# Regrouping batch 1's attention and moving two weight loads around the end of block 0

## The chip, the cores and the metric

The kernel runs on one core of one Trainium2 chip. The metric is the device time of one execution in microseconds (us), taken as the median of several runs. Traces come from one profiled execution.

## What is computed

A retention attention over q, k and v of shape (8 batches, 8 heads, 576 positions, 64), followed by a feed-forward layer with a sine-squared activation. The reference, cut to what matters:

```python
scores = scale * np.matmul(q, k.transpose(0, 1, 3, 2))
Dmat = np.where(rel >= 0, gamma[:, None, None] ** rel[None, :, :], 0.0)
attn = np.matmul(scores * Dmat[None], v)              # (8, 8, 576, 64)
x = attn.transpose(0, 2, 1, 3).reshape(8 * 576, 512)
h = x @ w_in                                          # 512 -> 2048
g = h + np.sin(alpha * h) ** 2 / (alpha + 1e-9)
out = g @ w_out                                       # 2048 -> 512
```

All inputs and the output are float32; the kernel computes in float16 with float32 sums.

## The kernel before, in words

**Blocks and units.** The 4608 tokens are worked in nine blocks of 512. Blocks 0 to 7 hold the first 512 positions of batches 0 to 7, and block 8 the last 64 of all. Each block goes through 16 *units*, one for each 128 of the 2048 hidden columns. A unit is `project` (four matmuls into one PSUM bank, line 541), `sine` on ACT (line 549), `square` on ACT, DVE or POOL (lines 558, 560) and `product` on DVE (line 565), which also frees the bank. Blocks 0 and 1 then multiply by w_out in 16 steps of four matmuls, `gemm2(n, u, bank)` (line 587): u // 4 is the group of 128 output rows and u % 4 the quarter of w_out that is read. `finish` copies a row group out of PSUM on ACT or DVE and stores it with two DMAs from SP (line 580). Later blocks use another scheme for the second product (`Quarters`), whose weight sums are made by `weigh` on POOL (line 608).

**Attention of a batch.** It works in two halves p of 256 positions. `load` brings 512 KB of float32 of q, k or v (line 121). `cast` scales and rounds it to float16: k and q by a multiplication with decay factors (line 181) on DVE or POOL, v by a copy (lines 102, 104). k and q are then transposed, either on PE (`turn`, line 215, with `take`, lines 102 and 104, out of PSUM) or by a DMA from SP (`crossed`, line 205). On PE, `outer` forms the sums of k times v (line 298), `scores` the products of k and q (line 363), `values` the product of masked scores with v in two parts (line 406), and `add_states` adds the carried state (line 428). All of these are 64x64 tiles, where the rest of PE's work is 128x128. DVE masks the scores (`masked`, line 375), ACT evicts the sums (`evict`, line 102), and POOL carries them on (`more`, lines 344 and 345; `to_state`, line 332). `keep` writes the block's x on ACT. `relay=` names an engine that passes on a mark between the two parts of `values`.

**What sets the order.** The whole order is written out by hand in one list (lines 746 to 1481), and each engine works off its own instructions in that order. Waits come only from data and from the reuse of buffers and banks. PSUM is taken by name: `h0`, `h1`, `h2` and `op` are single banks, `m0` and `m1` pairs. Raw loads share six buffers.

**Queues.** All loads of q, k and v, all DMA transposes and all stores are issued by SP (queue q1 in the profile). The weights are loaded by POOL (queue q0), with a conversion to float16 on the way: `load_w_in(g)` (line 92) and `load_w_out(g)` (line 95), one quarter of 512 KB after conversion each.

**Around the change.** Block 0's units 4 to 15 stand at lines 859 to 914. Between their steps, DVE casts batch 1's first k (lines 870, 878), PE turns it (line 895), and POOL issues the second quarter of w_out (line 866). Then block 0's gemm2 steps alternate with batch 1's attention (lines 915 to 981). POOL issues the third and fourth quarters of w_out at lines 929 and 930. From line 982 batch 2's q is cast and transposed, and block 1's units begin at line 994.

Of the kernel before, what the change touches and what calls it, by code (L numbers as in the profile page):

```python
# [18 lines left out]
def kernel(  # L19
# [68 lines left out]
    V, A_, G_ = nc.vector, nc.scalar, nc.gpsimd  # L88
# [5 lines left out]
    def load_w_out(g):  # L94
        nc.gpsimd.dma_start(w_out16[:, 4 * g : 4 * g + 4, :], w_out_r[:, 4 * g : 4 * g + 4, :])
# [42 lines left out]
    def cast(b, nm, p, eng, ys=(0, 1)):  # L138
        t_ = raw[b, nm, p]
        if (b, nm, p) not in half:  # L140
            if p < 2:
                if nm == "k":
                    d_ = work.tile([P, 16 * D], F16, tag=f"k16{slot(b, p)}", bufs=1, name="k16")
                elif nm == "q":
                    n = order_of_q.index((b, p)) % 3 if b < 5 else 1 - p
                    d_ = work.tile([P, 16 * D], F16, tag=f"q16{n}", bufs=1, name="q16")
                else:
                    d_ = work.tile([P, 16 * D], F16, tag="v16", bufs=4, name="v16")
                d_ = (
                    d_.rearrange("p (h r d) -> p h r d", r=2, d=D)  # L150
                    if nm == "v"
                    else d_.rearrange("p (a r t d) -> p a r t d", a=4, r=2, t=2)
                )
            elif nm == "v":
                d_ = work.tile([P, H, D], F16, tag="vs16", bufs=B // 2, name="vs16")
            else:
                tag, n = ("qks16", 2) if b % 4 == 0 else (f"k16{int(nm == 'q')}", 1)
                d_ = work.tile([P, 4, 2, D], F16, tag=tag, bufs=n, name=nm + "s16")
            half[b, nm, p] = d_
        dst = half[b, nm, p]  # L160
        if p == 2:
            if nm == "v":
                copy(eng, dst.rearrange("p h d -> p (h d)"), t_.rearrange("p h d -> p (h d)"))
            else:
                eng.tensor_tensor(
                    dst.rearrange("p a t d -> p t a d"),
                    t_.rearrange("p (t a) d -> p t a d", t=2),
                    fac_s[nm].rearrange("p (t a) -> p t a", t=2).unsqueeze(3).to_broadcast([P, 2, 4, D]),
                    MULT,
                )  # L170
        elif nm == "v":
            h0, h1 = 4 * ys[0], 4 * ys[-1] + 4
            copy(
                eng,
                dst[:, h0:h1].rearrange("p h r d -> p (h r d)"),
                t_[:, h0:h1].rearrange("p h x -> p (h x)"),
            )
        else:
            a0, a1 = 2 * ys[0], 2 * ys[-1] + 2
            n = 2 * (a1 - a0)  # L180
            return eng.tensor_tensor(  # L181
                dst[:, a0:a1].rearrange("p a r t d -> p t (a r) d"),
                t_.rearrange("p (t a) x -> p t a x", t=2)[:, :, a0:a1].rearrange("p t a (r d) -> p t (a r) d", r=2),
                fac["halved k" if nm == "k" and b >= HALVED else nm]
                .rearrange("p (t x) -> p t x", t=2)[:, :, 2 * a0 : 2 * a1]
                .unsqueeze(3)
                .to_broadcast([P, 2, n, D]),
                MULT,
            )
# [19 lines left out]
    def turn(b, nm, p, tag, ys=(0, 1)):  # L209
        if (b, nm, p) not in trs:  # L210
            trs[b, nm, p] = psum.tile([P, 1024], F16, tag=tag, bufs=1, name="tr")
        tr, x = trs[b, nm, p], half[b, nm, p]
        for a in range(2 * ys[0], 2 * ys[-1] + 2):
            for r in range(2):
                matmul(  # L215
                    tr[:, 256 * a + 128 * r : 256 * a + 128 * r + 128],
                    x[:, a, r].rearrange("p t d -> p (t d)"),
                    ident,
                    start=(a == 0 and r == 0), stop=True, is_transpose=True, skip_group_check=True,
                )  # L220

    def take(b, nm, p, eng, ys=(0, 1)):
        d_ = new_T(b, nm, p).rearrange("p x n -> p (x n)")
        cols = slice(512 * ys[0], 512 * ys[-1] + 512)
        copy(eng, d_[:, cols], trs[b, nm, p][:, cols])
# [307 lines left out]
    def project(n, fc, tag, part=None):  # L533

        if n not in gT:
            gT[n] = work.tile([P, 2, FC, 256], F16, tag="gT", bufs=2, name="gT")
        if (n, fc) not in hps_of:
            hps_of[n, fc] = [bank(tag), None]
        cols = PART[part]
        for a in range(KT):  # L540
            matmul(  # L541
                hps_of[n, fc][0][:, cols], w_in16[:, a, fc * P : (fc + 1) * P], xs[n][:, a, cols],
                start=(a == 0 and part != 1), stop=(a == KT - 1), skip_group_check=True,
            )
# [9 lines left out]
    def square(n, fc, eng):  # L554
        s_t = hps_of[n, fc][1]
        ss_t = work.tile([P, 512], F16, tag="ss", bufs=4, name="ss_t")
        if eng is nc.scalar:
            nc.scalar.activation(ss_t, s_t, mybir.ActivationFunctionType.Square)  # L558
        else:
            eng.tensor_tensor(ss_t, s_t, s_t, MULT)  # L560
        hps_of[n, fc][1] = ss_t

    def product(n, fc):
        hps, ss_t = hps_of.pop((n, fc))
        nc.vector.scalar_tensor_tensor(  # L565
            gT[n][:, :, fc, :], ss_t.rearrange("p (t n) -> p t n", t=2), inva[:, fc : fc + 1],
            hps.rearrange("p (t n) -> p t n", t=2), MULT, ADD,
        )
# [13 lines left out]
    def gemm2(n, u, tag, cols=slice(0, 512)):  # L582
        c, part = divmod(u, 4)
        if (n, c, cols.start) not in ops:
            ops[n, c, cols.start] = psum.tile([P, 512], F32, tag=tag, bufs=1, name="ops")
        for fk in range(4 * part, 4 * part + 4):
            matmul(  # L587
                ops[n, c, cols.start][:, cols], gT[n][:, c // 2, fk, c % 2 * P : c % 2 * P + P], w_out16[:, fk, cols],
                start=(fk == 0), stop=(fk == FC - 1), skip_group_check=True,
            )  # L590
# [102 lines left out]
    at = [Attention(b) for b in range(B)]  # L693
# [52 lines left out]
    with tc.manual_schedule():  # L746
# [116 lines left out]
        project(0, 5, "m0")  # L863
        sine(0, 5)
        square(0, 5, A_)
        load_w_out(1)
        project(0, 6, "op")
        product(0, 5)
        product(0, 4)
        cast(1, "k", 0, V, (0,))  # L870
        sine(0, 6)
        square(0, 6, G_)
        project(0, 7, "h2")
        sine(0, 7)
        square(0, 7, A_)
        product(0, 6)
        product(0, 7)
        cast(1, "k", 0, V, (1,))
        project(0, 8, "h0")
        sine(0, 8)  # L880
        square(0, 8, G_)
# [2 lines left out]
        square(0, 9, A_)  # L884
        product(0, 8)
        product(0, 9)
        project(0, 10, "m0")
        sine(0, 10)
        square(0, 10, G_)
        project(0, 11, "op")  # L890
        sine(0, 11)
        square(0, 11, V)
        product(0, 10)
        product(0, 11)
        turn(1, "k", 0, "m1")
        project(0, 12, "h2")
        sine(0, 12)
        square(0, 12, G_)
        take(1, "k", 0, V, (0,))
        take(1, "k", 0, V, (1,))  # L900
        project(0, 13, "h0")
        sine(0, 13)
        square(0, 13, A_)
        cast(1, "q", 0, G_)
# [15 lines left out]
        gemm2(0, 0, "h0")  # L920
        at[0].to_state(3, G_)
        at[1].scores(0, 0, "m0")
        gemm2(0, 5, "op")
        at[1].scores(0, 1, "m1")
        at[1].masked(0, 0)
        at[1].masked(0, 1)
        cast(1, "v", 0, G_, (0,))
        cast(1, "v", 0, A_, (1,))
        load_w_out(2)
        load_w_out(3)  # L930
        gemm2(0, 13, "h2")
        load(2, "k", 1)
        load(2, "k", 0)
        load(2, "q", 0)
        at[1].outer((0,), "m0")
        at[1].evict((0,), A_)
        cast(1, "k", 1, G_)
        at[1].values(0, False, "m1", relay=G_)
        gemm2(0, 1, "h0")
        at[1].to_state(0, G_)  # L940
        at[1].values(0, True)
        turn(1, "k", 1, "h1")
        cast(1, "q", 1, V)
        take(1, "k", 1, V)
        at[1].add_states(0)
        at[1].keep(0, A_)
        load(2, "v", 0)
# [14 lines left out]
        cast(2, "k", 0, V)  # L962
        crossed(2, 0, "k")
        gemm2(0, 9, "h1")
        at[1].outer((1,), "m0")
        at[1].evict((1,), A_)
        at[1].more(2)
        at[1].to_state(2, G_)
        gemm2(0, 6, "op")
        gemm2(0, 14, "h2")  # L970
        at[1].values(1, False, "m1", relay=A_)
        gemm2(0, 2, "h0")
        at[1].values(1, True)
        at[1].add_states(1)
        at[1].keep(1, A_)
        gemm2(0, 10, "h1")
        gemm2(0, 15, "h2")
        finish(0, 3, V)
        weigh(1, 1, G_)
        gemm2(0, 7, "op")  # L980
        finish(0, 1)
        cast(2, "q", 0, V)
        crossed(2, 0, "q")
        crossed(2, 1, "k")
        load(3, "k", 1)
        at[1].more(3)
        at[1].to_state(3, G_)
        cast(2, "v", 0, G_)
# [10 lines left out]
        sine(1, 1)  # L999
        gemm2(0, 3, "h0")  # L1000
        product(1, 0)
        finish(0, 0)
        square(1, 1, A_)
        project(1, 2, "m1", 0)
# [507 lines left out]
```

## Time and profile before

| | |
|---|---|
| median of 3 runs | 297.12 us (296.72 to 297.46) |
| the profiled execution | 295.89 us |
| its span, from the first to the last instruction | 294.2 us |
| granted TensorE clock | 0.998 |
| moved by DMA | 49.89 MB, mean 170 GB/s |
| mean of one sine, square (ACT), product | 682, 630, 743 ns |

The profiled execution's own time is a little longer than its span, and 1.23 us below the median. In the profile, PE is TensorE's matmuls, PEld its weight loads, DVE VectorE, ACT ScalarE, POOL GpSimd and SP SyncE; SPq and POOLq are their DMA issues. A row of a timeline has its start, its length, engine, line, operation and tiles, and in brackets the idle time before it and what ended that. A duration of a matmul group includes the tail of its last one, so the start of the next group is the better measure. The DMA view has packets, megabytes and the share of the sixteen DMA engines' time for each queue.

### The profile page before, as it was taken

The numbers are of one execution on the slowest core, as the hardware profiler recorded it, in microseconds if no ns is written. First come the engines' busy times: TensorE is split into PE (matmuls) and PEld (weight loads), VectorE is DVE, ScalarE is ACT, GpSimd is POOL, SyncE is SP. The second block draws the span as 40 slices with busy tenths as digits, with TensorE's granted clock in tenths as the row PEclk, the third lists the DMA queues.
The fourth block names the chain that finished last, engine by engine and source line by source line (L and its number), as shares of the span: only waits on it lengthen the run. The fifth ranks groups of instructions, "written<-read, shape, count | busy, mean of one in ns | idle before, by whom it ended". The sixth has DMA issues, their size and how long they took to land.

```text
span 294.2 us, 8759 instructions
## 1 busy us (share of the span) xinstructions
PE 281.9 (96%) x3607; PEld 184.4 (63%) x3607; DVE 217.9 (74%) x298; ACT 209.0 (71%) x339; POOL 210.1 (71%) x201
## 2 busy tenths in 40 slices
PE   7799999999989999999999999999999999999993
PEld 5474454576544676666666666666666666665782
DVE  3759976899568799989686867686777495747861
ACT  2859732886847898877787778787868879887600
POOL 4888889999999989999979799679816800460000
PEclk9999999999999999999999999999999999999999
DMA  7999999999999378978797877667647201311225
GB/s 221 293 248 222 269 208 283 246 190 271 243 254 293 74 174 181 259 166 203 158 263 166 194 194 204 110 135 178 137 111 188 44 2 39 72 38 28 58 47 119
DMA packets 119159, 49.89 MB, mean 170 GB/s; under 512 B 69824, under 2 KB 118096, under 8 KB 119120
## 3 DMA queue, kind: packets, MB, share of 16 engines
q1 hardware_dynamic: 114528, 45.04, 64.1%
q0 software_dynamic: 4224, 4.19, 8.5%
q8 instruction: 28, 0.46, 0.7%
q10 hardware_dynamic: 368, 0.11, 0.2%
q14 instruction: 11, 0.09, 0.1%
HBM read 36.74 MB, written 9.44 MB: 157 GB/s over the span
## 4 chain that ended last, share of the span: by engine, by line
PE 77%; POOL 8%; DMA 5%; DVE 4%; SPq 2%; ACT 2%; issue 1%; POOLq 0%; ACTq 0%
PE hps L541 35%; PE hps L658 29%; PE ops L587 4%; POOL T L608 4%; DMA q<-in_q_dram 4%; PE sc L363 2%; PE o L406 2%; SPq L121 2%; DMA qT<-q 1%; DVE gT L565 1%; PE kv L298 1%; POOL q L181 1%; DVE ret L375 1%; PE tr L215 1%; POOL v L104 1%
## 5 line engine op out<-in xcount | busy, mean ns | idle before, releaser
L565 DVE SCALAR_TENSOR_TENSOR gT<-ss_t,inva,hps 128x512 f16<-128x512 f16 x144 | 105.4, 743 | 38.7 <-ACT ss_t L558 37.2
L549 ACT ACTIVATE s_t<-hps,alpha_t 128x512 f16<-128x512 f32 x144 | 96.7, 682 | 38.0 <-PE hps L541 37.4
L541 PE MATMUL hps<-xT,w_in 128*128 128x512 f16 (+1 forms) x600 | 121.1, 348 | 0.4 <-DVE gT L565 0.4
L541 PEld LDWEIGHTS <-w_in 128*128 128x128 f16 x664 | 63.5, 98 | 50.4 <-issue 1.1
L558 ACT ACTIVATE ss_t<-s_t 128x512 f16<-128x512 f16 x118 | 73.9, 630 | 3.3
L658 PEld LDWEIGHTS <-gT 128*128 128x128 f16 x656 | 63.8, 98 | 14.5
L630 POOL TENSOR_TENSOR gT<-gT,d 128x1024 f16<-128x1024 f16 x12 | 25.6, 2151 | 26.1 <-PE hps L658 24.7
L658 PE MATMUL hps<-T,gT 128*128 128x256 f16 x336 | 39.8, 273 | 0.0
L375 DVE TENSOR_TENSOR ret<-sc,mask 128x1024 f16<-128x1024 f32 (+1 forms) x32 | 35.1, 1118 | 4.3 <-PE sc L363 4.1
L658 PE MATMUL hps<-w_out,gT 128*128 128x256 f16 x320 | 38.2, 273 | 0.0
L678 DVE TENSOR_TENSOR osb<-osb,hps 128x512 f32<-128x512 f32 x35 | 23.9, 684 | 11.9 <-PE hps L658 11.3
L587 PE MATMUL ops<-w_out,gT 128*128 128x512 f16 x128 | 31.2, 380 | 0.0
L181 POOL TENSOR_TENSOR q<-q,cn 128x1024 f16<-128x1024 f32 (+1 forms) x16 | 26.2, 1649 | 0.1
L636 POOL TENSOR_TENSOR gT<-gT 128x1024 f16<-128x1024 f16 x12 | 25.3, 2129 | 0.0
L345 POOL TENSOR_TENSOR kvs<-s,kvs 128x256 f32<-128x256 f32 x24 | 19.1, 797 | 2.5 <-ACT kvs L102 0.8
L587 PEld LDWEIGHTS <-gT 128*128 128x128 f16 x128 | 11.6, 98 | 12.4
L332 POOL TENSOR_TENSOR s<-kvs,cn 128x256 f16<-128x256 f32 x23 | 16.1, 703 | 4.1 <-ACT kvs L102 3.3
L102 ACT CAST xT<-o 128x1024 f16<-128x1024 f32 (+1 forms) x15 | 14.4, 966 | 6.6 <-PE o L428 6.6
L181 POOL TENSOR_TENSOR k<-k,cn 128x1024 f16<-128x1024 f32 (+1 forms) x11 | 18.8, 1713 | 0.0
L102 ACT COPY osb<-hps 128x512 f32<-128x512 f32 (+2 forms) x15 | 8.2, 550 | 13.5 <-PE hps L658 13.3
L560 DVE TENSOR_TENSOR ss_t<-s_t 128x512 f16<-128x512 f16 x19 | 13.4, 708 | 5.7 <-ACT s_t L549 5.6
L344 POOL TENSOR_TENSOR s<-kvs,cn 128x256 f32<-128x256 f32 x24 | 16.3, 678 | 0.2
(76 smaller groups left out, 272.3 us busy)
## 6 DMA issues: line engine op xcount, KB each, us to landing
out_dram<-osb SPq DMA_DIRECT2D x70, 128.0 KB, 2.5
q<-in_q_dram SPq DMA_DIRECT2D x16, 512.0 KB, 5.6
k<-in_k_dram SPq DMA_DIRECT2D x10, 512.0 KB, 6.8
v<-in_v_dram SPq DMA_DIRECT2D x10, 512.0 KB, 6.2
k<-in_k_dram SPq DMA_DIRECT2D x24, 128.0 KB, 3.6
v<-in_v_dram SPq DMA_DIRECT2D x24, 128.0 KB, 3.4
w_in<-in_moe_w_in_dram POOLq DMA_DIRECT2D x4, 512.0 KB, 9.4
w_out<-in_moe_w_out_dram POOLq DMA_DIRECT2D x4, 512.0 KB, 10.6
```

The costliest lines, as they stand in the source:

```text
L102: eng.copy(d_, s_)
L181: return eng.tensor_tensor(dst[:, a0:a1].rearrange("p a r t d -> p t (a r) d"), t_.rearrange("p (t a) x -> p t a x", t=2)[:, :, a0:a1].rea ...
L375: made = nc.vector.tensor_tensor(ret.rearrange("p t (z x) -> p (t z) x", z=2)[:, :, 0:n], sc.rearrange("p t (z x) -> p (t z) x", z=2)[:, : ...
L541: matmul(hps_of[n, fc][0][:, cols], w_in16[:, a, fc * P : (fc + 1) * P], xs[n][:, a, cols], start=(a == 0 and part != 1), stop=(a == KT - ...
L549: nc.scalar.activation(s_t, hps, mybir.ActivationFunctionType.Sin, bias=0.0, scale=alpha_t[:, fc : fc + 1],)
L558: nc.scalar.activation(ss_t, s_t, mybir.ActivationFunctionType.Square)
L565: nc.vector.scalar_tensor_tensor(gT[n][:, :, fc, :], ss_t.rearrange("p (t n) -> p t n", t=2), inva[:, fc : fc + 1], hps.rearrange("p (t n) ...
L587: matmul(ops[n, c, cols.start][:, cols], gT[n][:, c // 2, fk, c % 2 * P : c % 2 * P + P], w_out16[:, fk, cols], start=(fk == 0), stop=(fk ...
L630: eng.tensor_tensor(self.part(0, 0, i), self.part(1, 1, i), self.d3[:, 4 * i : 4 * i + 4], SUB)
L636: eng.tensor_tensor(out_, self.part(1, 0, i), self.part(0, 0, i), SUB)
L658: matmul(self.ps[name][:, 256 * m + cols.start : 256 * m + cols.stop], left(j)[:, P * m : P * m + P], right(j)[:, cols], start=(tag is not ...
L678: nc.vector.tensor_tensor(out_, a, self.ps[ps], ADD)
```

## The change

Nothing is computed differently; instructions change places in the list.

- Units 6 to 13 of block 0: `load_w_out(1)` goes from ahead of unit 6 to behind its square. The two casts of batch 1's first k move later on DVE, by two products each. `load_w_out(2)` goes from line 929 to behind unit 10's square. The turn of k goes from ahead of unit 12 to behind unit 13's projection.
- Batch 1's attention: the two `scores` of half 0 stand together; the cast of the second k stands ahead of the outer product; the first `to_state` goes ahead of a gemm2 step, and the second part of `values` of half 0 stands with its `add_states`; in half 1 one gemm2 step goes ahead of the outer product, which then stands with the first part of `values`.
- `finish(0, 3)` copies on ACT instead of DVE. Batch 2's first q is cast on DVE behind unit 0's product, and its transpose and the load of batch 3's second k move with it, behind the transpose of batch 2's second k.

```diff
-        load_w_out(1)
         project(0, 6, "op")
         product(0, 5)
         product(0, 4)
-        cast(1, "k", 0, V, (0,))
         sine(0, 6)
         square(0, 6, G_)
+        load_w_out(1)
         project(0, 7, "h2")
...
         product(0, 7)
-        cast(1, "k", 0, V, (1,))
+        cast(1, "k", 0, V, (0,))
...
         product(0, 9)
+        cast(1, "k", 0, V, (1,))
         project(0, 10, "m0")
         sine(0, 10)
         square(0, 10, G_)
+        load_w_out(2)
...
         product(0, 11)
-        turn(1, "k", 0, "m1")
...
+        project(0, 13, "h0")
+        turn(1, "k", 0, "m1")
         take(1, "k", 0, V, (0,))
         take(1, "k", 0, V, (1,))
-        project(0, 13, "h0")
...
         at[1].scores(0, 0, "m0")
-        gemm2(0, 5, "op")
         at[1].scores(0, 1, "m1")
         at[1].masked(0, 0)
         at[1].masked(0, 1)
+        gemm2(0, 5, "op")
         cast(1, "v", 0, G_, (0,))
         cast(1, "v", 0, A_, (1,))
-        load_w_out(2)
         load_w_out(3)
...
+        cast(1, "k", 1, G_)
         at[1].outer((0,), "m0")
         at[1].evict((0,), A_)
-        cast(1, "k", 1, G_)
         at[1].values(0, False, "m1", relay=G_)
+        at[1].to_state(0, G_)
         gemm2(0, 1, "h0")
-        at[1].to_state(0, G_)
-        at[1].values(0, True)
         turn(1, "k", 1, "h1")
         cast(1, "q", 1, V)
         take(1, "k", 1, V)
+        at[1].values(0, True)
         at[1].add_states(0)
...
         gemm2(0, 9, "h1")
+        gemm2(0, 6, "op")
         at[1].outer((1,), "m0")
         at[1].evict((1,), A_)
         at[1].more(2)
         at[1].to_state(2, G_)
-        gemm2(0, 6, "op")
+        at[1].values(1, False, "m1", relay=A_)
         gemm2(0, 14, "h2")
-        at[1].values(1, False, "m1", relay=A_)
         gemm2(0, 2, "h0")
...
-        finish(0, 3, V)
+        finish(0, 3)
         weigh(1, 1, G_)
         gemm2(0, 7, "op")
         finish(0, 1)
-        cast(2, "q", 0, V)
-        crossed(2, 0, "q")
         crossed(2, 1, "k")
-        load(3, "k", 1)
...
         product(1, 0)
+        cast(2, "q", 0, V)
+        crossed(2, 0, "q")
+        load(3, "k", 1)
         finish(0, 0)
```

## The prediction

> **What bounds the kernel now.** I read the page first: span, and busy time of each engine.
>
> ```profile
> span 294.2 us, 8759 instructions
> PE 281.9 (96%) x3607; PEld 184.4 (63%) x3607; DVE 217.9 (74%) x298; ACT 209.0 (71%) x339; POOL 210.1 (71%) x201
> ```
>
> PE is busy 96% of the span, so a change can only win what PE waits, and the edits all lie between 24 and 57 us. The busy time by stretches shows who else is full behind them:
>
> ```profile
> 46.00:74.00 28.00, 27.30 (x378) 17.45 (x380) 23.42 (x30) 18.57 (x32) 27.25 (x28) 1.00 1.09 251
> 74.00:88.00 14.00, 12.76 (x233) 6.83 (x222) 8.15 (x11) 9.19 (x16) 13.73 (x14) 1.00 1.13 244
> 96.00:290.00 194.00, 192.99 (x2367) 131.83 (x2364) 146.20 (x204) 147.73 (x235) 126.25 (x101) 1.00 0.57 132
> ```
>
> The columns are the stretch, its length, then PE, PEld, DVE, ACT, POOL, PE's clock, DMA share, GB/s. POOL has 27.25 of 28 us and then 13.73 of 14, so it hardly pauses from 46 to 88 us. From 96 us on PE has 192.99 of 194: whatever PE is late by at 88 us stays to the end. So the question is what sets PE's arrival at 88 us. PE's timeline shows its three waits there:
>
> ```profile
> 73.02 1.38 PE L406 MATMUL o<-ret,v 64*64 64x128 f16 x64 [0.61 <-DVE ret L375]
> 80.20 0.64 PE L363 MATMUL sc<-qT,kT 64*64 64x128 f16 x32 [0.29 <-DMA qT<-q]
> 87.08 0.64 PE L363 MATMUL sc<-qT,kT 64*64 64x128 f16 x32 [0.95 <-DMA qT<-q]
> ```
>
> At 80.20 and 87.08, batch 3's scores wait for transposed q, 0.29 + 0.95 = 1.24 us in all. In the timelines of POOL and SP I followed this back:
>
> ```profile
> 74.74 1.90 POOL L181 TENSOR_TENSOR q<-q,cn 128x1024 f16<-128x1024 f32 x1
> ...
> 76.66 1.41 SPq L205 DMA_TRANSPOSE qT<-q  x1
> 78.13 0.58 SPq L121 DMA_DIRECT2D q<-in_q_dram  x1
> 78.76 0.56 SPq L121 DMA_DIRECT2D k<-in_k_dram  x1
> 79.42 3.10 SPq L205 DMA_TRANSPOSE kT<-k  x1
> 82.63 2.12 SPq L205 DMA_TRANSPOSE qT<-q  x1
> ```
>
> POOL ends the cast of batch 3's second q at 76.64, SP issues its transpose at 76.66, and from there SP's list runs without a pause to the transpose at 82.63 that PE awaits at 87.08. Before 74.74 POOL's line is unbroken, and its last wait is this one, for batch 1's second outer product (through ACT's eviction):
>
> ```profile
> 46.20 0.73 POOL L345 TENSOR_TENSOR kvs<-s,kvs 128x256 f32<-128x256 f32 x1 [0.59 <-ACT kvs L102]
> 47.01 1.48 POOL L332 TENSOR_TENSOR s<-kvs,cn 128x256 f16<-128x256 f32 x1
> ...
> 51.66 1.68 POOL L344 TENSOR_TENSOR s<-kvs,cn 128x256 f32<-128x256 f32 x1
> ```
>
> So the end hangs on a chain: outer product at 44.97, POOL from 46.20, SP from 76.66, PE at 87.08. PE's own work before that has 1.24 us to spare. I price every edit by what it does to the outer product.
>
> **Part by part.** *Casts of k and unit groups (25 to 33 us).* Here are a wait of PE, and the DVE casts:
>
> ```profile
> 27.99 1.02 PE L541 MATMUL hps<-xT,w_in 128*128 128x512 f16 x4 [0.42 <-DVE gT L565]
> ...
> 26.21 1.06 DVE L181 TENSOR_TENSOR k<-k,cn 128x512 f16<-128x512 f32 x1
> 28.51 0.68 DVE L181 TENSOR_TENSOR k<-k,cn 128x512 f16<-128x512 f32 x1
> ```
>
> The first cast stands ahead of the product that frees the bank of unit 11; moved behind it, the 0.42 us goes. But both casts still stand ahead of units 10 and 11 on DVE, so unit 13 and the turn of k wait a little instead: I keep 0.2 us, between 0 and 0.4. Batch 1's attention has nine groups of 64-wide matmuls now and six after it (I count the turns apart): scores 0 joined, values and states of half 0 joined, outer product and values of half 1 joined. A gemm2 step takes 0.95 us by start times ahead of such a group (42.27 to 43.22, below) and 0.87 where one follows another (2.60 for three, next rows), so three groups save 0.3 us of PE.
>
> ```profile
> 49.07 2.76 PE L587 MATMUL ops<-w_out,gT 128*128 128x512 f16 x12
> 51.67 1.90 PE L541 MATMUL hps<-xT,w_in 128*128 128x256 f16 x12
> ```
>
> Neither gain reaches the end by itself, since PE waits at 87.08 anyway.
>
> *The outer product of half 1.* PE now:
>
> ```profile
> 41.65 0.62 PE L215 MATMUL tr<-ident,q 128*128 128x128 f16 x8
> 42.27 1.02 PE L587 MATMUL ops<-w_out,gT 128*128 128x512 f16 x4
> 43.22 0.64 PE L363 MATMUL sc<-qT,kT 64*64 64x128 f16 x32
> 43.79 1.04 PE L587 MATMUL ops<-w_out,gT 128*128 128x512 f16 x4
> 44.97 0.45 PE L298 MATMUL kv<-v,k 64*64 64x64 f16 x32
> ```
>
> From the turn of the second q (41.65) to the outer product (44.97) are 3.32 us, with a wait of about 0.3 before the latter (43.79 + 0.87 = 44.66) for the bank that DVE's mask holds. The change puts another gemm2 step (0.87) there: 44.66 + 0.87 + 0.10 of switching = 45.6, so the stretch becomes 3.95 us. POOL's chain loses 0.63 us by that alone.
>
> *The third quarter of w_out, issued about 5 us sooner.* This is the term I weigh most. The DMA view by stretches (packets, MB, share), for 27 to 32 us (a quarter under way), 34 to 37 (none), 0 to 34, then 33 to 34 and 39 to 40:
>
> ```profile
> q0 software_dynamic: 706, 0.71, 83.2%
> q1 hardware_dynamic: 704, 0.35, 34.9%
> ...
> q1 hardware_dynamic: 1942, 0.98, 109.4%
> ...
> q1 hardware_dynamic: 10029, 5.06, 53.8%
> ...
> q0 software_dynamic: 55, 0.04, 25.4%
> ...
> q0 software_dynamic: 62, 0.06, 40.9%
> ```
>
> q1 is SP's queue with all loads of q, k and v; q0 is POOL's with the weights. Alone, q1 moves 0.98 / 3 = 0.33 MB/us; beside a quarter, 0.07, packet for packet with q0, which moves 0.14. A quarter (0.52 MB) thus takes 3.7 us and lets q1 do 0.26 MB in place of 1.2: it costs the loads behind it 2.9 us. Issues on POOL:
>
> ```profile
> 28.98 1.11 POOL L560 TENSOR_TENSOR ss_t<-s_t 128x512 f16<-128x512 f16 x1 [0.78 <-ACT s_t L549]
> ...
> 35.34 1.55 POOL L95 DMA_DIRECT2D w_out<-in_moe_w_out_dram  x2
> ```
>
> Now the third quarter is issued at 35.34 and its packets come after 39, when batch 1's loads are done. After the change it is issued behind the square that ends at 30.09; with the same 3.5 to 4 us it starts at about 34, just as the second quarter drains (55 packets left at 33). (The second quarter, issued at about 26.4 in place of 24.84, still queues behind the first: I cost that at nothing; a gap in q0 would only pass time to q1.) The twelve loads of batches 0 and 1 are 0.524 MB each, and batch 1's second q is the eleventh: it has come when q1 has moved 5.77 MB. At 34.0 it has moved 5.06, so 0.71 is left. Today that takes 2.2 us (36.2 as a mean over the engines; the last a little later), and the cast did not wait for it:
>
> ```profile
> 39.06 1.21 DVE L181 TENSOR_TENSOR q<-q,cn 128x1024 f16<-128x1024 f32 x1
> ```
>
> After: 34.0 to 37.7 gives 0.26 MB; then q1 is alone until the fourth quarter starts (issued at about 35.1, so 38.6): 0.30 MB; the last 0.15 MB goes beside that quarter at 0.07: 40.8 as a mean, and I take 42.1 for the last engine. Cast to 43.3, turn of q at 43.3 instead of 41.65: 1.65 us. Bounds: a load there by 40.4 costs nothing (40.4 + 1.21 = 41.6); one that sits out the whole fourth quarter on the slowest engine lands at 43.5 and costs 3.1. The cast of k (the tenth load) starts at 38.9 rather than 36.90 and ends at 40.9, when PE reaches its turn today; inside the same delay.
>
> *Second q of unit 0, and the order on SP.* The cast of batch 2's q leaves DVE's place at 51.64 for one behind two products, and its transpose goes behind that of the second k:
>
> ```profile
> 51.64 1.23 DVE L181 TENSOR_TENSOR q<-q,cn 128x1024 f16<-128x1024 f32 x1
> ...
> 57.36 1.29 SPq L205 DMA_TRANSPOSE qT<-q  x1
> 58.70 2.46 SPq L205 DMA_TRANSPOSE kT<-k  x1
> ```
>
> The two swap places, so qT comes 1 to 2.5 us later. With PE about 2 us later itself, batch 2's scores meet it; without that PE would wait 0 to 1.5 us there, inside its 1.24 to spare. I take 0. The load of batch 3's second k moves with it on SP, to about the place it has in time today. The output copy of row 3 moves from DVE to ACT, which idled there: nothing.
>
> [...]
>
> **Sum.** 1.65 + 0.63 = 2.28 us on the outer product, then on POOL, SP and PE at 87.08. The profiled execution took 295.89 us, so 298.2; the median of the runs lies 1.23 above it: 299.4.
>
> **Rivals.** (1) *The quarters miss the loads* (the early one starts after 37, or the fourth after the eleventh load). Only the extra gemm2 step is left, less 0.1 of PE's lead: 297.12 + 0.5 = 297.6. For it: my landing times are means over sixteen engines, with 1.3 us added for the last. Against: packets alternate as soon as both queues have work.
> (2) *Faster: POOL is released from DVE's casts.* POOL's step at 51.66 took 1.68 us against 0.62 for the same step uncontended (44.99 us, below), and 51.64 to 52.87 is just the DVE cast that leaves; the one at 47.01 took 1.48 under another cast. If both shrink, POOL wins 1.06 + 0.8 = 1.9, and with loads in time PE gets at most its 1.24: 295.9. It decides if the outer product slips under 0.9 us. Against: the casts still run, and can block POOL elsewhere.
>
> ```profile
> 44.99 0.62 POOL L344 TENSOR_TENSOR s<-kvs,cn 128x256 f32<-128x256 f32 x1
> ```
>
> [...]
> (3) *Slower still*: the second q sits out the whole fourth quarter, 3.1 + 0.63, and qT's swap adds some: 301.
>
> **How the numbers follow.** Forecast 0.52, (1) 0.20, (2) 0.18, (3) 0.10. About 0.3% (0.9 us) is what a measurement of this kernel can tell from no change: faster 0.18, same 0.20, slower 0.62. The range, 296.3 to 301.2, leaves out most of (2) and the end of (3).
>
> **What would show it.** In the changed profile: q0 and q1 sharing from 34 to 38 us; DVE's cast of batch 1's second q waiting on DMA past 41; the outer product of half 1 at about 47, POOL's L345 behind it, scores of batch 3 near 89.4. PE's 0.42 us at 28 should be gone. I am wrong if that cast does not wait, or if POOL's line from 46 on is shorter than today's 30.4 us to the cast's end at 76.64.

## The result and the profile after

| | before | after |
|---|---|---|
| median | 297.29 us (296.71 to 298.06, 6 runs) | 301.26 us (300.34 to 301.67, 6 runs) |
| profiled execution, its span | 295.89, 294.2 us | 301.63, 299.9 us |
| granted TensorE clock over the span | 0.998 | 0.993 |

The change makes the kernel slower: the ratio is 1.0138, with a 95% interval of 1.0118 to 1.0158, or 3.97 us by the medians. The forecast was 299.4 us with a range up to 301.2. The sign was right; in the kernel as it ran, most of the loss comes from somewhere else than the prediction said.

The page of the kernel after, its first line and the busy times:

```profile
span 299.9 us, 8758 instructions
PE 283.7 (95%) x3607; PEld 184.8 (62%) x3607; DVE 225.9 (75%) x297; ACT 210.3 (70%) x340; POOL 209.9 (70%) x201
```

DVE lost a copy to ACT (297 instructions, not 298), and yet it is busy 8.0 us longer (225.9 against 217.9). PE is busy 1.8 us longer with the same 3607 matmuls. Both are signs that single instructions became longer, so DVE's timeline comes first. Kernel after, DVE:

```profile
29.81 0.68 DVE L181 TENSOR_TENSOR k<-k,cn 128x512 f16<-128x512 f32 x1
30.41 4.48 DVE L560 TENSOR_TENSOR ss_t<-s_t 128x512 f16<-128x512 f16 x1
34.82 1.39 DVE L565 SCALAR_TENSOR_TENSOR gT<-ss_t,inva,hps 128x512 f16<-128x512 f16 x2
...
44.04 1.22 DVE L181 TENSOR_TENSOR q<-q,cn 128x1024 f16<-128x1024 f32 x1
```

The square of unit 11 takes 4.48 us. In the kernel before the same instruction stands at the same time and takes a tenth of that:

```profile
30.43 0.41 DVE L560 TENSOR_TENSOR ss_t<-s_t 128x512 f16<-128x512 f16 x1
```

POOL's timeline of the kernel after, over the same stretch:

```profile
28.78 1.04 POOL L560 TENSOR_TENSOR ss_t<-s_t 128x512 f16<-128x512 f16 x1 [0.77 <-ACT s_t L549]
29.77 0.80 POOL L95 DMA_DIRECT2D w_out<-in_moe_w_out_dram  x1
30.59 1.05 POOL L560 TENSOR_TENSOR ss_t<-s_t 128x512 f16<-128x512 f16 x1
31.59 1.90 POOL L181 TENSOR_TENSOR q<-q,cn 128x1024 f16<-128x1024 f32 x1
33.45 0.61 POOL L332 TENSOR_TENSOR sS<-kvs,cn 128x256 f16<-128x256 f32 x1
34.01 0.60 POOL L104 CAST v<-v 128x512 f16<-128x512 f32 x1
34.56 0.80 POOL L95 DMA_DIRECT2D w_out<-in_moe_w_out_dram  x1
...
38.80 1.89 POOL L181 TENSOR_TENSOR k<-k,cn 128x1024 f16<-128x1024 f32 x1 [3.44 <-DMA k<-in_k_dram]
```

In the kernel before, POOL paused for 1.28 us ahead of unit 12's square, until ACT's sine was ready at 31.30:

```profile
31.37 1.04 POOL L560 TENSOR_TENSOR ss_t<-s_t 128x512 f16<-128x512 f16 x1 [1.28 <-ACT s_t L549]
```

Two things closed that pause. The turn of k no longer stands ahead of unit 12's projection, so the sine is ready at 29.88; and the issue of the third w_out quarter runs from 29.77 to 30.57. Unit 12's square now starts 0.10 us after DVE's cast ends (30.49), and four arithmetic instructions follow each other until 34.61. DVE's square ends 0.28 us later, at 34.89. Its row shows no wait on a semaphore; the time is inside the instruction.

PE needs the bank that DVE's next product frees. Kernel after, PE:

```profile
30.78 1.03 PE L541 MATMUL hps<-xT,w_in 128*128 128x512 f16 x4
35.61 1.21 PE L541 MATMUL hps<-xT,w_in 128*128 128x512 f16 x4 [3.80 <-DVE gT L565]
36.62 3.44 PE L587 MATMUL ops<-w_out,gT 128*128 128x512 f16 x8
...
40.34 1.03 PE L587 MATMUL ops<-w_out,gT 128*128 128x512 f16 x4
...
50.22 0.45 PE L298 MATMUL kv<-v,k 64*64 64x64 f16 x32
...
86.64 0.64 PE L363 MATMUL sc<-qT,kT 64*64 64x128 f16 x32 [0.26 <-DVE gT L565]
...
92.50 0.64 PE L363 MATMUL sc<-qT,kT 64*64 64x128 f16 x32
```

Two losses stand here: the wait of 3.80 us, and behind it eight matmuls that take 3.28 us by start times (36.62 to 39.90). Kernel before, the same steps:

```profile
32.94 1.89 PE L587 MATMUL ops<-w_out,gT 128*128 128x512 f16 x8
34.66 0.61 PE L215 MATMUL tr<-ident,q 128*128 128x128 f16 x8
35.11 1.03 PE L587 MATMUL ops<-w_out,gT 128*128 128x512 f16 x4
```

There they took 1.72 (32.94 to 34.66). The busy times by stretches of the kernel after say why (columns as in the prediction, PE's clock third from the end):

```profile
31.00:36.00 5.00, 1.20 (x6) 0.41 (x5) 5.00 (x3) 1.44 (x4) 4.36 (x5) 1.00 1.20 216
36.00:40.00 4.00, 4.00 (x13) 1.47 (x12) 3.51 (x7) 1.92 (x3) 1.20 (x1) 0.57 1.18 253
```

PE did only 1.20 us of work from 31 to 36, and then its clock was 0.57 on average from 36 to 40. So the step at 40.34 is 5.23 us later than before's 35.11; the outer product of half 1 is 5.25 later (50.22 against 44.97), the last scores of batch 3 5.42 (92.50 against 87.08), and the span 5.7. Those scores wait for nothing, where before's waited 0.95 us for transposed q: here PE itself is late, and not the chain through POOL and SP. The medians differ by 3.97: before's profiled execution is a short one (295.89, and its median 297.29), after's lies 0.37 above its median. Of the runs told below one execution (of run 14: 418.63 us, at a clock of 0.659) was disturbed and is left out.

The DMA part of the prediction also came true, and yet cannot be seen in the end: POOL's cast of k waited for its load until 38.80 (forecast 38.9). But DVE's cast of the second q at 44.04 waited for nothing: DVE and PE were late already. So there were two candidates for the loss, one hiding the other.

### The profile page after: what moved, and what is told of

It reads as the page before. It is cut to its first block, busy times and chain, and to the rows that moved or that the text cites. A ratio compares the mean times of both kernels' runs of the same rounds, so it can differ in the third digit from the quotient of the medians.

```text
span 299.9 us, 8758 instructions
## 1 busy us (share of the span) xinstructions
PE 283.7 (95%) x3607; PEld 184.8 (62%) x3607; DVE 225.9 (75%) x297; ACT 210.3 (70%) x340; POOL 209.9 (70%) x201
## 4 chain that ended last, share of the span: by engine, by line
PE 79%; DVE 9%; POOL 5%; ACT 4%; issue 2%; POOLq 0%; ACTq 0%; DVEq 0%
PE hps L541 35%; PE hps L658 28%; PE ops L587 7%; PE sc L363 3%; DVE gT L565 2%; PE o L406 2%; ACT s_t L549 2%; DVE ret L375 2%; POOL T L608 2%; PE kv L298 2%; DVE k L181 1%; DVE ss_t L560 1%; PE idle L702 1%; POOL q L181 1%; PE tr L215 1%
## 5 line engine op out<-in xcount | busy, mean ns | idle before, releaser
L587 PE MATMUL ops<-w_out,gT 128*128 128x512 f16 x128 | 32.5, 394 | 0.0
L181 POOL TENSOR_TENSOR q<-q,cn 128x1024 f16<-128x1024 f32 (+1 forms) x16 | 27.0, 1701 | 0.4 <-DMA q<-in_q_dram 0.3
L560 DVE TENSOR_TENSOR ss_t<-s_t 128x512 f16<-128x512 f16 x19 | 18.5, 973 | 9.5 <-ACT s_t L549 9.4
```

The costliest lines, as they stand in the source:

```text
L181: return eng.tensor_tensor(dst[:, a0:a1].rearrange("p a r t d -> p t (a r) d"), t_.rearrange("p (t a) x -> p t a x", t=2)[:, :, a0:a1].rea ...
L587: matmul(ops[n, c, cols.start][:, cols], gT[n][:, c // 2, fk, c % 2 * P : c % 2 * P + P], w_out16[:, fk, cols], start=(fk == 0), stop=(fk ...
```

## The experiments

The theory at this point: **the issue took POOL's pause, POOL's unbroken arithmetic kept DVE's square out, PE waited and lost its clock.** The first rival: **the third quarter makes the second q late**, as predicted. Others: the regrouped attention, batch 2's q.

Each ratio below is to the kernel before, measured beside the runs; its median there was 296.99, 296.62, 296.89 and 296.59 us for runs 1 to 4, 5 to 8, 9 to 12 and 13 to 15.

**1. The square of unit 11 on ACT.** The kernel after with

```diff
-        square(0, 11, V)
+        square(0, 11, A_)
```

> The changed kernel with unit 11's square on ACT instead of DVE. In the changed kernel that square took 4.48 us on DVE (0.41 before) while POOL ran without a pause, PE waited 3.80 us behind it and then had 0.57 of its clock for 4 us. Theory A (DVE's square is locked out by POOL's run, and that is the loss): the square takes about 0.63 us on ACT, PE's 3.80 us wait is gone, the clock stays at 1.00, and 3 us or more of the 4.0 come back: 297.3 to 298.3. Theory B (the weight quarter delays batch 1's loads, as predicted): PE's wait at unit 15 goes, but the cast of batch 1's second q then waits on its load past 41 us and the time stays near 299.4.

301.27 us (299.58 to 302.6), ratio 1.0147 (1.0098 to 1.0196): no gain. But it isn't the same loss. PE, then DVE:

```profile
40.89 0.62 PE L215 MATMUL tr<-ident,k 128*128 128x128 f16 x8 [0.79 <-POOL k L181]
...
44.61 1.03 PE L215 MATMUL tr<-ident,q 128*128 128x128 f16 x8 [2.64 <-DVE q L181]
45.43 1.91 PE L587 MATMUL ops<-w_out,gT 128*128 128x512 f16 x4
```

```profile
43.05 1.50 DVE L181 TENSOR_TENSOR q<-q,cn 128x1024 f16<-128x1024 f32 x1 [4.39 <-DMA q<-in_q_dram]
```

The stall at 35 is gone. PE now runs into the late loads, waits 0.79 + 2.64 us, and the clock halves again (four matmuls in 1.91 us at 45.43, instead of 1.03). In this version the late loads alone cost as much as the held square and the late loads together.

**2. The third quarter back ahead of the fourth.** The kernel after with

```diff
         square(0, 10, G_)
-        load_w_out(2)
...
+        load_w_out(2)
         load_w_out(3)
```

> The changed kernel with the third quarter of w_out issued at its old place, ahead of the fourth. If the issue on POOL is what locks DVE's square out, the square is short again and the time is near 297.3. If POOL's squares and casts alone already leave no pause (unit 12's square is ready at 29.9 us in the changed kernel, and DVE's square starts at 30.4), the square still takes 2 to 3 us or more, and the time stays at 299.5 or above. Theory B: the loads are back in time, 297.4.

297.85 us, ratio 1.003 (1.0016 to 1.0045). This one edit carries about 3 of the 4 us. Something is left, and the rows of DVE and POOL show it:

```profile
31.35 1.26 DVE L560 TENSOR_TENSOR ss_t<-s_t 128x512 f16<-128x512 f16 x1
```

```profile
29.72 2.61 POOL L560 TENSOR_TENSOR ss_t<-s_t 128x512 f16<-128x512 f16 x2 [0.77 <-ACT s_t L549]
```

The square is still held, 0.85 us over its 0.41, and PE waits 0.58 us for it. POOL's squares of units 10 and 12 follow each other almost at once, with no issue between them: the new order of the units alone takes most of the 1.28 us of pause.

A caution on start times: in this profiled execution TensorE's clock was already 0.5 from 8.97 to 12.38 us, ahead of all the edits, and block 0's units begin about 0.9 us later than in the kernel after. The profiled executions of runs 8 and 10 have such a stretch too (from 14.10 and 8.96). It doesn't make up the rest of the loss: run 2's executions with a mean clock of 0.996 or more took 297.55 to 297.86 us.

**3. The third quarter alone.** The kernel before with

```diff
         square(0, 10, G_)
+        load_w_out(2)
...
-        load_w_out(2)
         load_w_out(3)
```

> The kernel before with only the third quarter issued early, behind unit 10's square. Theory B: k's cast on POOL waits to about 38.9 us and the cast of the second q waits on its load to about 42: 298.5 to 299.5. Theory A: unit 11's square on DVE waits for POOL's issue to end, at most 0.9 us, since unit 12's square starts only at 31.4 and leaves a pause: 297.3 to 298.0.

297.25 us, ratio 1.0012 (0.9993 to 1.0031). DVE, then PE:

```profile
30.17 0.42 DVE L560 TENSOR_TENSOR ss_t<-s_t 128x512 f16<-128x512 f16 x1
41.67 1.41 DVE L181 TENSOR_TENSOR q<-q,cn 128x1024 f16<-128x1024 f32 x1 [2.79 <-DMA q<-in_q_dram]
```

```profile
40.91 0.62 PE L215 MATMUL tr<-ident,k 128*128 128x128 f16 x8 [0.24 <-POOL k L181]
...
43.14 0.62 PE L215 MATMUL tr<-ident,q 128*128 128x128 f16 x8 [1.35 <-DVE q L181]
...
46.44 0.45 PE L298 MATMUL kv<-v,k 64*64 64x64 f16 x32
```

Here is the predicted mechanism by itself: the load lands at 41.67 (forecast 42.1), the turn of q comes 1.49 us late (forecast 1.65), the outer product 1.47. The median moves by only 0.26 us, though the profiled execution's span is 1.7 us longer than before's. And POOL's issue, here from 29.78 to 30.58, does not hold the square, which ran at full speed inside it. In before's order the sine that POOL's next square needs comes later (POOL starts it at 31.13), so a pause of 0.54 us was left behind the issue.

**4. The regrouped attention alone.** The kernel before with the part of the diff from `at[1].scores(0, 0, "m0")` to `gemm2(0, 2, "h0")`, with both quarters issued together as before.

> The kernel before with only batch 1's attention regrouped, all else in its old place. My sum has 0.63 us of delay on the outer product of half 1, less 0.2 to 0.3 us that PE saves in groups: 297.6. If the regrouping were the loss, 299 or more; if PE's savings counted in full, 296.9.

296.86 us, ratio 0.9997 (0.9973 to 1.0021): no change. PE waits, since the step that went ahead of the outer product reads the third quarter:

```profile
45.27 1.02 PE L587 MATMUL ops<-w_out,gT 128*128 128x512 f16 x4 [1.02 <-DMA w_out<-in_moe_w_out_dram]
46.22 0.45 PE L298 MATMUL kv<-v,k 64*64 64x64 f16 x32
...
87.77 0.64 PE L363 MATMUL sc<-qT,kT 64*64 64x128 f16 x32 [1.77 <-DMA qT<-q]
```

The outer product is 1.25 us later, and that costs nothing that can be told in the median; the last scores are 0.69 later. POOL makes up 1 us of it: from its step behind the outer product to the end of the cast of batch 3's second q it takes 29.45 us (47.46 to 76.91), where before it took 30.44.

**5 and 6. Work in POOL's pause.** The kernel before, with two products (5) or one (6) on POOL that change nothing:

```diff
         square(0, 10, G_)
+        nc.gpsimd.tensor_tensor(zero, zero, zero, MULT)
+        nc.gpsimd.tensor_tensor(zero, zero, zero, MULT)
```

> The kernel before with two extra POOL products of 128x512 float16 (a scratch tile squared in place, not part of the computation) behind unit 10's square, so that POOL has no pause from 29 to 36 us; nothing else is moved. Theory A (DVE's square of unit 11 is locked out as long as POOL runs without a pause): the square, 0.41 us in the kernel before, takes 4 us or more, PE waits 3 us or more for a bank at unit 15 or the first gemm2, its clock falls, and the time is 300 or more. If instead the early quarter or the new order is needed for the loss: the square waits at most one POOL instruction (1.04 us) and the time is 297.0 to 298.

> The kernel before with one such extra POOL product (30.1 to 31.1 us), so that a pause of about 0.2 us stays before unit 12's square at 31.4. Theory A: DVE's square gets in at the pause, about 0.7 us late, and the time is 297.0 to 297.8. If the extra POOL work by itself cost the time: about half of what two cost.

297.26 us, ratio 1.0023 (0.9997 to 1.0049), and 297.1, 1.0016 (0.9993 to 1.004). The square took 0.94 us in both: a hold for the one instruction that ran, with no cost that can be told. As a test of the long hold run 5 missed: the second product waits for the first, which leaves a pause of 0.08 us between them (30.86 to 30.93), and there the square got in. The run of arithmetic wasn't unbroken.

**7. Matmuls in PE's wait, first attempt.** The kernel after, with 16 matmuls of zeros ahead of unit 15, into the spare half of unit 10's pair of banks (`spare`):

```diff
+        for _ in range(16):
+            matmul(spare["m0"][:, 1], zero[:, 0:P], zero, start=True, stop=True, skip_group_check=True)
         project(0, 15, "m0")
```

> The changed kernel with 16 extra matmuls (zeros, into an unused bank, not part of the computation) ahead of unit 15, where PE waits 3.80 us. If PE's slow clock afterwards (0.57 from 36 to 40 us) comes from that wait: the clock stays at 1.00, the first gemm2 steps take 0.87 us again in place of 1.70, and the time falls by about 1.5 us, to 299.8. If the slow clock has another cause, or if the lost 1.5 us are hidden behind the loads of batch 1 anyway: 301.0 to 301.5.

305.28 us, ratio 1.0292 (1.0232 to 1.0352). A miss: the added matmuls themselves waited 3.80 us, since they write the tile that the late product reads. They then took 5.31 us for 16, which take 3.62 at full clock (run 11), and the steps behind them ran at full speed. So the slow clock isn't bound to certain matmuls: it lies on whatever follows the wait.

**8. The second quarter back as well.** Run 1 with `load_w_out(1)` at its old place:

```diff
         square(0, 5, A_)
+        load_w_out(1)
         project(0, 6, "op")
...
         square(0, 6, G_)
-        load_w_out(1)
```

> The changed kernel with unit 11's square on ACT and the second quarter of w_out issued at its old place; the third stays early. If the later second quarter pushes the third and so the loads (my prediction cost it at nothing): the cast of batch 1's second q ends its wait about 1.4 us sooner than in the run with the square on ACT alone (41.7 in place of 43.05), PE's wait at its turn falls to about 1.4 us, its clock holds, and the time is 297.5 to 298.5. If the second quarter's place costs nothing: 301.

299.47 us (297.79 to 300.11), ratio 1.0078 (1.0046 to 1.011), against 1.0147 (1.0098 to 1.0196) for run 1. The later second quarter seems to cost 1 to 2 us when the third stands close behind it. The intervals overlap, and the times are spread over 2.3 us, so this stays a lead. Its profiled execution is its fastest, and no example of the median.

**9. Both mendings.** Run 2 with the square of unit 11 on ACT.

> The kernel after with both mendings at once: unit 11's square on ScalarE, the third w_out quarter back ahead of the fourth. If the held square and the late second q are the two losses, and each only hid the other, both go: no PE wait over 0.7 us between 30 and 45 us, the second q cast without waiting for its load, the outer product of half 1 at about 46, and 297.0 to 297.8 us (ratio 1.000 to 1.002 to before). If the regrouped attention or batch 2's q carries a loss of its own, 298 us or more stays.

296.42 us (295.69 to 298.11), ratio 0.9994 (0.9969 to 1.0019). DVE, then PE:

```profile
38.23 1.22 DVE L181 TENSOR_TENSOR q<-q,cn 128x1024 f16<-128x1024 f32 x1
```

```profile
44.41 0.41 PE L298 MATMUL kv<-v,k 64*64 64x64 f16 x27
```

The cast of q waits for nothing, the outer product is even 0.56 us sooner than before's, and the whole loss is gone. The rest of the change (groups, casts, batch 2's q) costs nothing that can be measured. It brings nothing either: this version is not distinguishable from the kernel before.

**10. POOL without its pause, nothing added.** The kernel before with

```diff
         square(0, 10, G_)
+        cast(1, "q", 0, G_)
...
         square(0, 12, G_)
...
-        cast(1, "q", 0, G_)
```

> The kernel before, with GpSimd's cast of batch 1's first q (1.90 us) taken out from behind unit 12's square and put behind unit 10's, in the pause of 1.28 us: nothing is added, only the pause goes. If a square of VectorE can be held through a whole run of GpSimd's instructions, unit 11's square takes 3 to 4.5 us from 30.4 instead of 0.41, PE waits over 2.5 us, and the time is 299.5 to 301.3 us. If it is held for no more than the one instruction that runs, it takes at most 2.1 us, PE waits about 1.2 us, and the time is under 298.0 us.

298.08 us (296.83 to 299.71), ratio 1.003 (0.9999 to 1.0061). DVE, then POOL:

```profile
31.17 1.80 DVE L560 TENSOR_TENSOR ss_t<-s_t 128x512 f16<-128x512 f16 x1
```

```profile
30.80 1.90 POOL L181 TENSOR_TENSOR q<-q,cn 128x1024 f16<-128x1024 f32 x1
32.65 1.22 POOL L560 TENSOR_TENSOR ss_t<-s_t 128x512 f16<-128x512 f16 x1
```

The square asks while the cast runs, and ends 0.28 us behind it, at 32.97; POOL's own square is stretched from 1.04 to 1.22. So it was held for one instruction and got in at the seam to the next, with no pause there that the rows show. My theory of "the whole unbroken run" does not hold in general.

**11. Matmuls in PE's wait, second attempt.** The kernel after, with the matmuls of zeros into a bank that is free:

```diff
+        keep_busy(16, "h1")
         project(0, 14, "h1")
```

> The kernel after with 16 matmuls of zeros into a free bank ahead of unit 14's projection (3.46 us at full clock), so that TensorE has work while VectorE's square is held; the rest is as in after. If the wait of 3.8 us is what brings the clock of 0.5, the slow stretch at 36.3 goes, the eight matmuls of gemm2 take about 1.75 us instead of 3.28, the outer product of half 1 comes at about 49.0 instead of 50.22, and the time is 299.8 to 300.8 us. If the slow clock has another cause, or if what it costs is hidden behind the second q, the time stays at 301 to 301.6 us.

300.39 us (300.21 to 300.93), ratio 1.0108 (1.0076 to 1.0139), 0.87 us less than the kernel after, with more work; the two intervals overlap (after's ratio is 1.0138, 1.0118 to 1.0158), so the traces are the better evidence. PE, then DVE:

```profile
30.73 3.62 PE L702 MATMUL idle<-zero 128*128 128x512 f16 x16
...
36.44 2.12 PE L587 MATMUL ops<-w_out,gT 128*128 128x512 f16 x8
...
49.12 0.45 PE L298 MATMUL kv<-v,k 64*64 64x64 f16 x32
```

```profile
30.36 4.49 DVE L560 TENSOR_TENSOR ss_t<-s_t 128x512 f16<-128x512 f16 x1
...
43.31 1.22 DVE L181 TENSOR_TENSOR q<-q,cn 128x1024 f16<-128x1024 f32 x1 [0.68 <-DMA q<-in_q_dram]
```

The hold is the same, but the clock stays at full speed, and the eight matmuls' row is 2.12 us instead of 3.44. The outer product gains 1.10 us. Now the cast of q waits 0.68 us for its load: the second loss shows from behind the first as soon as that shrinks.

**12. Batch 2's q alone.** The kernel before with the eviction of `finish(0, 3)` on ACT, and `cast(2, "q", 0, V)`, `crossed(2, 0, "q")` and `load(3, "k", 1)` behind `product(1, 0)`.

> The kernel before with only the last part of the change: the eviction of block 0's last quarter on ScalarE, batch 2's first q cast and turned behind unit 0 of block 1, the load of batch 3's k behind it. Theory: 296.8 to 297.6 us, no change, the transposes of that q no later than they are needed. Rival: what the kernel after still loses with its third quarter back (0.3%) comes from here: 297.9 to 298.5 us.

297.03 us, ratio 0.9994 (0.9974 to 1.0014): nothing, as the theory had it.

**13 to 15. Why the square is held so long.** Three versions of the kernel after. In 13, six empty instructions (`nc.gpsimd.nop()`) stand behind the issue of the third quarter; in 14, the issue of the fourth stands sooner; in 15, two products of eight columns stand where 13 has the empty ones. Their diffs in this order:

```diff
         load_w_out(2)
+        for _ in range(6):
+            nc.gpsimd.nop()
```

```diff
         cast(1, "q", 0, G_)
+        load_w_out(3)
...
-        load_w_out(3)
```

```diff
         load_w_out(2)
+        nc.gpsimd.tensor_tensor(zero[:, 0:8], zero[:, 0:8], zero[:, 0:8], MULT)
+        nc.gpsimd.tensor_tensor(zero[:, 0:8], zero[:, 0:8], zero[:, 0:8], MULT)
```

> The kernel after with six empty instructions on GpSimd between the issue of the third w_out quarter and unit 12's square. If VectorE's square is held because GpSimd starts 0.1 us behind it with no gap, these push GpSimd's square back by 0.1 to 0.4 us, VectorE's goes first and takes 0.41 us (or 1.3 us if it waits for one instruction), PE waits less than 1 us there, the second q is then waited for to 43, and the time is near 301.3 us as with the square on ScalarE. If the issue itself is what holds VectorE, or if the empty instructions take no time, it stays at about 4.5 us and 301.3 us.

> The kernel after with the issue of the fourth w_out quarter moved up behind the cast of batch 1's first q, two arithmetic instructions (0.61 us each) sooner. If VectorE's square is held until GpSimd leaves arithmetic for an issue, it ends at about 33.8 and takes 3.3 us instead of 4.48, and PE waits 2.6 us instead of 3.8. If the hold has a length of its own or ends at a point further down, it stays at 4.48 us.

> As the first of these, with two small products (8 columns, in place, the second waiting for the first) in the place of the six empty instructions, which certainly take some tenths of a microsecond and have a pause between them. If a pause of a tenth of a microsecond is enough for VectorE, its square takes 0.4 to 0.8 us and PE's wait falls under 1 us. If the issue holds it, 4.5 us stay.

Run 13 tells nothing: the empty instructions took no time, POOL's square started 0.02 us behind the issue as in the kernel after, DVE's took 4.49 us, and the time was 300.92 us (two runs).

Run 14, 300.78 us (one execution). DVE, then POOL:

```profile
30.52 3.77 DVE L560 TENSOR_TENSOR ss_t<-s_t 128x512 f16<-128x512 f16 x1
```

```profile
31.71 1.90 POOL L181 TENSOR_TENSOR q<-q,cn 128x1024 f16<-128x1024 f32 x1
33.55 0.81 POOL L95 DMA_DIRECT2D w_out<-in_moe_w_out_dram  x1
```

The square ends inside the issue that cuts POOL's arithmetic short, 0.7 us sooner in its length than in the kernel after, and PE waits 3.10 us. I had expected 3.3 us for the square; it ends 0.7 us behind the cast rather than 0.3, and I can't say why. But the hold has no fixed length: it ended sooner where POOL left arithmetic sooner, in this one trace.

Run 15, 298.24 us (297.9 to 299.98), ratio 1.0058 (1.0026 to 1.0089). POOL, then DVE:

```profile
30.73 0.28 POOL L891 TENSOR_TENSOR zero<-zero 128x8 f16<-128x8 f16 x1
31.09 0.20 POOL L892 TENSOR_TENSOR zero<-zero 128x8 f16<-128x8 f16 x1
31.25 1.04 POOL L560 TENSOR_TENSOR ss_t<-s_t 128x512 f16<-128x512 f16 x1
```

```profile
30.55 0.41 DVE L560 TENSOR_TENSOR ss_t<-s_t 128x512 f16<-128x512 f16 x1
...
41.20 1.70 DVE L181 TENSOR_TENSOR q<-q,cn 128x1024 f16<-128x1024 f32 x1 [2.46 <-DMA q<-in_q_dram]
```

Half a microsecond of useless work on POOL gives back more than half of the loss (the ratio falls from 1.0138 to 1.0058): the square takes 0.41 us again. What is left, 1.65 us by the medians, goes with the late q: the loss that was predicted.

**What follows.** The loss of the kernel after is made by the place of one issue within the new order, in two ways. The place by itself is not enough: in before's order it costs 0.26 us, which can't be told from nothing (run 3). And the order without it costs 0.86 us (run 2). On POOL, the issue puts unit 12's square 0.10 us behind the moment at which DVE's square of unit 11 is ready; that one is held for 4.48 us, PE waits 3.80 and then runs 3.41 us at half clock. On the DMA queues the quarter makes the second q late. Runs 1 and 15 leave only the second, run 11 a smaller first, run 2 a small rest of the first; run 9 leaves neither and is level with before.

What stays open is the rule by which DVE gets in. It was held over several instructions when it asked 0.10 us before POOL's square began, with POOL in a transfer's issue (after, 7, 11, 13 and 14), and got in behind the first when it asked while POOL's arithmetic was running (2, 5, 6 and 10). In run 15 it asked 0.11 us before a short product of POOL and wasn't held. So neither "until POOL pauses" nor "for one instruction" covers all runs.

Nor is it settled why the late q costs 4.28 us in run 1 and 1.65 in run 15, but two things on record bear on it. The load ended at 43.05 in the one and at 41.20 in the other, though the quarter was issued at 29.96 and 29.91; what differs is the fourth quarter's issue, at 34.78 and 35.23. In runs 11, 1, 3 and 15 it came at 34.52, 34.78, 35.12 and 35.23, and the load ended at 43.31, 43.05, 41.67 and 41.20. And a stretch of 3.41 us at half clock lowers the mean clock of an execution by 0.006: all four executions of run 1 have a mean of 0.986 to 0.991, while four of run 15's seven have 0.996 to 1.000 and took 297.93 to 298.34 us. The profiled one, with its slow stretch, took 299.73. So run 1 probably pays for lost clock every time, and run 15's median does not.

## Why the prediction was wrong

- **What failed: the term "Casts of k and unit groups", put at 0 to 0.4 us of gain, which left out what POOL's issue does to DVE's square.** The part on the third quarter put its issue "behind the square that ends at 30.09" and followed its packets, but not the 0.80 us that the issue takes on POOL, nor who used POOL's pause: the square of unit 11 on DVE at 30.43. The gain itself came as forecast: the wait of 0.42 us at unit 11 went, and one of 0.18 at unit 13 came, 0.24 in all for a forecast of 0.2. But beside it stood 3.80 us of wait and 1.56 of slow clock (3.28 - 1.72); less the 0.24, that makes 5.12 of the 5.23 us at the next step. This mechanism stood among no rival.
- **The contention of DVE and POOL, which I looked for only in POOL's steps (rival 2: 1.68 us against 0.62), bears on DVE's as well.** In runs 5, 6 and 10 the square took 0.94, 0.94 and 1.80 us: held for one instruction of POOL. In the kernel after it was ready 0.10 us before POOL's own square began, and still it took 4.48 us, over four instructions of POOL. A hold of one instruction, as in those three runs, would not have given the loss.
- **The third quarter on the DMA queues: right in mechanism; its size held in two settings and not in the third.** k's cast at 38.80 (forecast 38.9); q's load at 41.67 and 41.20 in runs 3 and 15, at 43.05 in run 1 (forecast 42.1, upper bound 43.5). The turn of q is 1.49 us late in run 3 and 1.31 in run 15 (forecast 1.65), but 2.96 in run 1 (44.61 against 41.65), where PE's clock fell as well and the outer product is 4.71 late (49.68). In the medians these runs cost 0.26, 1.65 and 4.28 us. That run 15's median loses the predicted 1.65 to the digit is luck: run 3 delays the same turn by more and costs 0.26.
- **"I cost that at nothing" for the second quarter's place is in doubt.** Run 8 against run 1 suggests 1 to 2 us in that setting.
- **The extra gemm2 step ahead of the outer product: right in size, wrong in effect.** From the turn of q to the outer product are 3.82 us in the kernel after (46.40 to 50.22), where I said 3.95, from 3.32. Run 4 has its outer product 1.25 us later at no cost that can be told (its interval allows 0.6 us at most), so the 0.63 us of the sum was too much.
- **Delay carried 1:1 to the end: true of PE behind 88 us, not of the chain and not of the median.** From the last scores of batch 3 to the end of the span are 207.1 us before and 207.4 after. But POOL's line, taken as rigid, gives way: from its step behind the outer product to the end of the cast it took 30.44 us before, 29.45 in run 4 and 29.16 after (51.46 to 80.62). And I took the slack from a profiled execution 1.23 us below its median, and added the whole delay to the median; run 4 shows that at least half of 1.25 us at the outer product can vanish there. No trace shows a typical execution of the kernel before, so what sets its time stays open.
- **Batch 2's q and the copy on ACT at nothing: right** (run 12), and rival 2, the faster one, did not show: run 12 has the cast away from POOL's steps and gains nothing (its line from 46.39 to the cast's end at 76.99 is 30.60 us).
- **Of the signs I named**, POOL's wait and PE's 0.42 us were as said; "DVE's cast of batch 1's second q waiting on DMA past 41" was missing after (44.04, without a wait), which I had named as what would prove me wrong. It was hidden rather than absent, as run 1 shows. The other such sign, a line of POOL shorter than 30.4 us, did appear (29.16). The outer product came at 50.22, not 47, and the scores at 92.50, not 89.4.

## What to carry to other kernels

An issue of a transfer is also an instruction on its engine (0.80 us of POOL in this kernel): before moving one into a pause, look which other engine works undisturbed in that pause and what else the change brings closer; here VectorE lost ten times what its instruction takes (4.48 us against 0.41). When one edit causes two delays on the same consumer, mending one shows nothing; mend both, then each alone. And read slack from several executions: the profiled one may be the one in which all was on time.

## What was not expected of the hardware

- A DVE square of 128x512 in float16 (0.41 us) took 4.48 us beside four successive POOL instructions of arithmetic, with no semaphore in its row; 0.94 to 1.80 beside one. POOL's issue of a transfer (0.80 us) did not hold it: 0.42 us inside one (run 3).
- After waits of 3.80 us (after and 7), 3.81 (13), 3.10 (14), 2.64 (1) and 1.16 (15), TensorE's clock was 0.5 for 3.41 us (36.34 to 39.75 in the kernel after), whatever it ran: there eight matmuls took 3.28 us by start times instead of 1.72, in run 7 sixteen of zeros 5.31 instead of 3.62 (run 11). It was not after 0.24 + 1.35 (run 3: 1.00 from 40 to 50 us), not after 1.77 (run 4, at 87.77, where the scores took 0.64 us as in the kernel before), and not when zeros were multiplied in the wait (run 11: 1.00 from 31 to 44 us). In runs 14 and 1 the slow stretch began before the wait ended (34.72 against 35.02, 43.83 against 44.61). How much waiting it takes isn't settled: 0.54 + 1.16 us in run 15 were followed by such a stretch, 0.24 + 1.35 in run 3 and 1.77 in run 4 were not, and in runs 2, 8 and 10 one came in the first 15 us (from 8.97, 14.10 and 8.96). No run shows why the stretch is 3.41 us long.
